# Storing the first block's results in 16 transfers instead of 64, and the last eight stores from two queues

## The chip, the cores and the metric

The kernel runs on one core of a Trainium2 chip. The metric is the device time of one execution in microseconds (us). TensorE (PE) multiplies matrices, VectorE (DVE) and ScalarE (ACT) do elementwise work and move results out of PSUM, GpSimd (POOL) does some additions, SyncE (SP) issues nearly all DMA transfers. An issue is an instruction in the queue of the engine that makes it: what stands behind it in that queue waits until it has been issued. The 16 DMA engines then move the bytes.

## The reference

Linear attention over 8 batches of 8 heads, an RMS norm, and two pairs of dense layers over the 4608 tokens, all in float32:

```python
kv = np.einsum('bhsd,bhse->bhde', k, v)          # batch 8, heads 8, seq 576, head_dim 64
out = np.einsum('bhsd,bhde->bhse', q, kv)
rms = np.sqrt(np.mean(out * out, axis=-1, keepdims=True) + 1e-06)
x = out / rms * g_norm                            # to [4608, 512]
h = x @ w_in                                      # [512, 2048]
x = where(h >= 1, h, where(h <= -1, 0, (h + 1) ** 2 / 4)) @ w_out
h = np.maximum(x @ w_in2, 0.0)
return (h * h) @ w_out2                           # [4608, 512]
```

The weights arrive in 64 bits and are narrowed to float32 on the chip.

## The kernel before

Every product is made of three products of rounded halves (a high and a low part, `mm3`, `mm_group`), so that float32 accuracy comes out of faster matmuls. The tokens are cut into nine blocks of 512: one of each batch (512 of its 576 rows), and block 8 of the 64 rows that are left of each batch.

The first layer pair runs block by block (`h_stage`, `g_stage`, `out_stage`). Its results go to DRAM tensors `x1d`. The second layer pair takes blocks 0 to 7 in four pairs, n = 0 to 3, each as a 2x2 product with seven instead of eight block products. A pair has two phases: `in_phase(n)` (tiles `ph`, 28 weight tiles, 12 matmuls each) and `out_phase(n)` (tiles `po`). Block 8 runs at the end like a block of the first layer pair.

The weight tiles of the second layer pair (`ws`, 512 KB each) are read from DRAM into a ring of eight buffers. `take_w2` takes a tile for the matmuls and calls `load_w2` (line 669), which issues the load seven tiles ahead on SyncE; the load waits until TensorE is through with the tile whose buffer it fills.

The results of a pair are stored while the next pair's `in_phase` runs: the list `late` has four calls of `put_out(n, hn, hm)`, which are made at steps 0, 1, 5 and 9 of that phase. `hn` says which block of the pair, `hm` which half of its 512 columns. Each call transposes two result tiles on DVE (line 885) into a tile `ov` and stores it from SyncE, 32 rows of output columns at a time. In block 0 the tokens stand in another order than in the others (row 4p + c of the batch is token p of group c, because its q, k and v were loaded that way), and so its stores differ: line 894 has 32 transfers of 16 KB for each call, line 901, for all other blocks, eight of 64 KB. The tile `ov` comes from `t_ring`, a ring of five buffers, of which `out_phase` takes its operands `t` as well: an operand that gets a buffer back from an `ov` waits until its stores have been written.

The order in each queue follows the program text, with a scheduler that moves instructions by their expected readiness; the names in the rows below are those of the tiles.

At the end, `out_stage(2, 8, 15)` copies four results from PSUM, two on DVE (line 601) and two on ACT (line 603), and each is stored in two halves of 64 rows by line 618 from SyncE.

Of the kernel before, what the change touches and what calls it, by code (L numbers as in the profile page):

```python
# [73 lines left out]
def linear_attention_rms_two_mlps(  # L74
# [12 lines left out]
    nc = tc.nc  # L87
    B, H, S, D = q.shape
    NT, DM = out.shape
    DFF = w_in1.shape[1] // 2  # L90
    P = 128
    NP = H // 2
    KD = DM // P
    NF = DFF // P
    TB = 512
    MR = TB // P
    REM = S - TB
    U = S // 2
    NB = NT // TB
# [88 lines left out]
    def mm3(dst, wt, xt, first, last):  # L188

        for n, (a, c) in enumerate(((0, 0), (0, 1), (1, 0))):  # L190
            nc.tensor.matmul(dst, wt(a), xt(c), start=first and n == 0, stop=last and n == 2)  # L191
# [391 lines left out]
    def out_stage(L, b, f):  # L583
        t = gs.pop((L, b, f))
        w = wo[L, f]
        if f == 0:
            acc[L, b] = [
                ps_a.tile([P, TB], F32, tag=f"acc{c}", name=f"acc{L}_{b}_{c}") for c in range(KD)
            ]
        for c in range(KD):  # L590
            s = slice(c * P, (c + 1) * P)
            if L == 1:
                lhs, rhs = (lambda a: w[:, a, s]), (lambda a: t[:, a, :])
            else:
                lhs, rhs = (lambda a: t[:, a, s]), (lambda a: w[:, a, :])
            mm3(acc[L, b][c], lhs, rhs, f == 0, f == NF - 1)
        if f == NF - 1:
            for c, a in enumerate(acc.pop((L, b))):
                t = st.tile([P, TB], F32, tag="st", name=f"ev{L}_{b}_{c}")
                if c % 2 == 0:  # L600
                    nc.vector.tensor_copy(t, a)
                else:
                    nc.scalar.copy(t, a)
                store(L, b, c, t)

    def store(L, b, c, t):
        if L == 1:
            nc.sync.dma_start(x1d[b][:, c, :], t)
        elif b == 0:

            nc.sync.dma_start(out[:TB, :].rearrange("(p c) f -> p c f", c=MR)[:, c, :], t)
        elif b < B:
            r0 = b * S + c * P
            nc.sync.dma_start(out[r0 : r0 + P, :], t)
        else:
            for j in range(P // REM):
                r0 = (c * (P // REM) + j) * S + TB
                nc.sync.dma_start(out[r0 : r0 + REM, :], t[j * REM : (j + 1) * REM, :])

    x_st = {}  # L620

# [257 lines left out]
    def put_out(n, hn, hm):  # L879


        t = t_ring.tile([P, 2, TB], F32, f"ov{n}_{hn}_{hm}")
        b = 2 * n + hn
        for m in range(2):
            nc.vector.transpose(t[:, m, :], result[n](hm, m, hn))
            d0 = (2 * hm + m) * P
            cols = out[b * S : b * S + TB, d0 : d0 + P]
            if b == 0:

                for c in range(MR):  # L890
                    for a in range(MR):
                        rows = cols.rearrange("(b i c) (a j) -> c a i b j", c=MR, i=32, j=32)
                        src = t[a * 32 : (a + 1) * 32, m, c * P : (c + 1) * P]
                        nc.sync.dma_start(  # L894
                            rows[c, a], src.rearrange("p (b j) -> p b j", j=32)
                        )
            else:
                for a in range(MR):
                    rows = cols.rearrange("(b i) (a j) -> a i b j", i=32, j=32)
                    src = t[a * 32 : (a + 1) * 32, m, :]  # L900
                    nc.sync.dma_start(rows[a], src.rearrange("p (b j) -> p b j", j=32))

    blocks = [(1, b) for b in range(NB)]
    hooks = {}
# [38 lines left out]
    for j in range(2 * NH):  # L943
        which, i = j % 2, j // 2
# [67 lines left out]
    for t in range(N1):  # L1012
        h_stage(*step(t))
        for f, a in hooks.get((t, 0), []):
            f(*a)
        g_stage(*step(t))
        if t >= LAG:
            out_stage(*step(t - LAG))
        for f, a in hooks.get((t, 1), []):
            f(*a)  # L1020

    late = []
    for n in range(NS):
        step_in = in_phase(n)
        for i, _ in enumerate(step_in):
            if n == 0 and i < LAG:
                out_stage(*step(N1 - LAG + i))
            if late and i in (0, 1, 5, 9):
                late.pop(0)()
        while late:  # L1030
            late.pop(0)()
        result[n] = result_of(dict(g2))
        jobs = x2_jobs(n + 1, tmp) if n + 1 < NS else x2_whole_jobs(2, NB - 1)
        at = range(8, 8 + 2 * len(jobs), 2)
        for _ in out_phase(n, jobs, at):
            pass
        late = [lambda n=n, h=h: put_out(n, h // 2, h % 2) for h in range(4)]

    L, b = 2, NB - 1
    for t in range(NF + LAG):  # L1040
        if t < NF:
            wi[L, t] = take_w2(0, t)
            h_stage(L, b, t)
        if late:
            late.pop(0)()
        if t < NF:
            g_stage(L, b, t)
        if t >= LAG:
            wo[L, t - LAG] = take_w2(1, t - LAG)
            out_stage(L, b, t - LAG)  # L1050
# [36 lines left out]
```

## Time and profile before

| | |
|---|---|
| median of 3 runs | 1629.64 us (1629.54 to 1631.46) |
| profiled execution | 1629.64 us, span from the first to the last instruction 1627.9 us |
| PE busy | 1593.7 us (98%), 7208 matmuls |
| DVE, ACT, POOL busy | 987.0 us (61%), 914.9 us (56%), 114.6 us (7%) |
| DMA | 302.31 MB, mean 186 GB/s |
| stores of line 901 | 112 of 64 KB, median 3.7 us from issue to landing |
| stores of line 894 | 64 of 16 KB, 1.5 us |
| stores of line 618 | 8 of 128 KB, 2.3 us |

Matmuls are pipelined, so the busy time of PE says that it hardly stands still, not how well it is used. Idle time of another engine costs nothing as long as PE does not wait for it. In the rows, `SPq` and `ACTq` are the queues of SyncE and ACT from which transfers are issued; the time beside such a row is that of the issue, and the landing is counted from its start.

### The profile page before, as it was taken

Reading aid. Unit: us, or ns where it says so; the run is one execution under the profiler, and the core shown is the slowest. Engines: PE = TensorE matmul, PEld = TensorE weight load, DVE = VectorE, ACT = ScalarE, POOL = GpSimd, SP = SyncE. Lnnn points to the kernel's source line nnn. Section 1 sums busy time; section 2 is a strip of 40 time slices with the busy share of each in tenths; the row PEclk is TensorE's granted clock in tenths of the full one; section 3 lists DMA queues with packets and bytes.
Section 4 is the critical chain, followed back from the end, with each engine's and each line's share of the span. In section 5 each row is a group of like instructions: output and inputs, shape, how many; then the busy total and the mean of one; then the engine's idle time right before and its main releaser. Section 6 shows DMA issues by size and latency. Waiting matters only on the chain.

```text
span 1627.9 us, 20609 instructions
## 1 busy us (share of the span) xinstructions
PE 1593.7 (98%) x7208; PEld 1312.0 (81%) x7208; DVE 987.0 (61%) x1638; ACT 914.9 (56%) x1661; POOL 114.6 (7%) x105
## 2 busy tenths in 40 slices
PE   8999999999999999999999999979999999999998
PEld 4778888888888888888888888868888888888886
DVE  6998665866757576443244348734875497457522
ACT  5777666766667666554344456436654664564321
POOL 0000000000000000000000121012101210230000
PEclk9999999999999999999999999989999999999999
DMA  9925668586667747313141457548758676865683
GB/s 264 276 93 156 212 182 263 161 251 184 196 198 223 231 148 238 112 56 104 39 144 38 156 194 245 194 119 257 246 192 225 208 241 198 241 220 184 193 246 102
DMA packets 307734, 302.31 MB, mean 186 GB/s; under 512 B 196272, under 2 KB 249520, under 8 KB 307632
## 3 DMA queue, kind: packets, MB, share of 16 engines
q1 hardware_dynamic: 305888, 300.61, 60.2%
q8 instruction: 57, 0.93, 0.2%
q10 hardware_dynamic: 1744, 0.39, 0.1%
q14 instruction: 45, 0.37, 0.1%
HBM read 231.74 MB, written 69.21 MB: 185 GB/s over the span
## 4 chain that ended last, share of the span: by engine, by line
PE 75%; issue 10%; DVE 9%; ACT 3%; DMA 1%; SPq 1%; POOL 1%; DVEq 0%; POOLq 0%; ACTq 0%
PE ph L191 26%; PE acc L191 25%; PE ph L737 11%; PE po L737 7%; DVE t L682 3%; PE pkv L403 2%; DVE x L682 1%; PE po L191 1%; PE pr L503 1%; SPq L894 1%; DVE g L827 1%; DMA ws<-wsd 1%; POOL t L798 1%; DVE xr L705 1%; DMA xr<-x1d 1%
## 5 line engine op out<-in xcount | busy, mean ns | idle before, releaser
L191 PE MATMUL ph<-x,w 128*128 128x512 f32 x1728 | 424.4, 394 | 9.5 <-ACT x L170 4.5
L191 PEld LDWEIGHTS ph<-x,w 128*128 128x128 f32 x1728 | 322.2, 189 | 78.9 <-ACT x L170 5.7
L737 PE MATMUL ph<-x,ws 128*128 128x512 f32 x1344 | 308.2, 391 | 11.0 <-DMA ws<-wsd 10.4
L737 PE MATMUL po<-t,ws 128*128 128x512 f32 x1344 | 307.4, 390 | 1.5 <-DVE t L682 1.5
L737 PEld LDWEIGHTS ph<-x,ws 128*128 128x128 f32 x1344 | 253.0, 189 | 65.2 <-issue 10.8
L737 PEld LDWEIGHTS po<-t,ws 128*128 128x128 f32 x1344 | 251.4, 188 | 56.9 <-DVE t L682 4.7
L191 PE MATMUL acc<-gs,w 128*128 128x512 f32 x1152 | 280.6, 391 | 0.3 <-DVE gs L184 0.2
L191 PEld LDWEIGHTS acc<-gs,w 128*128 128x128 f32 x1152 | 214.2, 188 | 44.4 <-DVE gs L184 1.4
L569 ACT ACTIVATE u<-ph,halfb 128x512 f32<-128x512 f32 x144 | 99.2, 689 | 205.1 <-PE ph L191 204.9
L571 DVE SCALAR_TENSOR_TENSOR u<-u,ph 128x512 f32<-128x512 f32 x144 | 98.6, 685 | 159.6 <-ACT u L178 158.9
L682 DVE TENSOR_TENSOR t<-g,t 128x512 fp32r<-128x512 f32 x192 | 135.3, 711 | 85.1 <-ACT t L170 69.3
L170 ACT CAST t<-g 128x512 fp32r<-128x512 f32 x192 | 116.4, 621 | 71.8 <-DVE t L682 50.1
L184 DVE TENSOR_TENSOR gs<-u,gs 128x512 fp32r<-128x512 f32 x160 | 110.4, 691 | 59.7 <-ACT gs L170 58.6
L191 PE MATMUL acc<-gs,wt 128*128 128x512 f32 x576 | 139.4, 391 | 0.0
L170 ACT CAST gs<-u 128x512 fp32r<-128x512 f32 x160 | 99.3, 621 | 69.7 <-DVE u L571 53.8
L191 PEld LDWEIGHTS acc<-gs,wt 128*128 128x128 f32 x576 | 106.8, 188 | 21.3
L790 DVE TENSOR_TENSOR h<-ph,e 128x512 f32<-128x512 f32 x96 | 66.1, 691 | 56.4 <-PE ph L737 50.7
L791 ACT ACTIVATE h<-h 128x512 f32<-128x512 f32 x96 | 60.5, 630 | 60.2 <-DVE h L790 56.0
L178 ACT ACTIVATE u<-u 128x512 f32<-128x512 f32 x144 | 91.0, 632 | 2.2
L798 POOL TENSOR_TENSOR t<-g 128x512 f32<-128x512 f32 x32 | 43.1, 1348 | 645.6 <-ACT g L792 365.0
L792 ACT ACTIVATE g<-h 128x512 f32<-128x512 f32 x128 | 80.9, 632 | 3.5
L782 DVE TENSOR_TENSOR e<-ph,e 128x512 f32<-128x512 f32 x64 | 43.4, 689 | 44.8 <-PE ph L737 43.7
(109 smaller groups left out, 1511.9 us busy)
## 6 DMA issues: line engine op xcount, KB each, us to landing
ws<-wsd SPq DMA_DIRECT2D x224, 512.0 KB, 3.4
wsd<-s SPq DMA_DIRECT2D x112, 256.0 KB, 3.9
wt<-wtd SPq DMA_DIRECT2D x48, 512.0 KB, 4.7
raw<-in_moe_w_in_dram SPq DMA_DIRECT2D x32, 512.0 KB, 5.2
raw<-in_moe_w_out_dram SPq DMA_DIRECT2D x32, 512.0 KB, 5.3
wcd<-s SPq DMA_DIRECT2D x32, 512.0 KB, 3.6
ws<-wcd SPq DMA_DIRECT2D x32, 512.0 KB, 4.3
x1d<-ev SPq DMA_DIRECT2D x36, 256.0 KB, 3.4
```

Source lines behind the costliest of these rows:

```text
L170: e.copy(dst, src)
L178: e.activation(dst, src, AF.Square)
L184: engine(op + "_lo", phase).tensor_tensor(t[:, 1, :], src, t[:, 0, :].bitcast(F32), ALU.subtract)
L191: nc.tensor.matmul(dst, wt(a), xt(c), start=first and n == 0, stop=last and n == 2)
L569: nc.scalar.activation(u, ps, AF.Relu, bias=halfb, scale=0.5)
L571: nc.vector.scalar_tensor_tensor(u, u, 1.0, ps, op0=ALU.min, op1=ALU.max)
L682: engine2(op + "_lo").tensor_tensor(t[:, 1, :], src, t[:, 0, :].bitcast(F32), ALU.subtract)
L737: nc.tensor.matmul(ps, wt(a), xt(c), start=first and n == 0 and i == 0, stop=last and n == len(lhs) - 1 and i == 2, skip_group_check=True,)
L790: nc.vector.tensor_tensor(h, bank, add, ALU.add)
L791: nc.scalar.activation(h, h, AF.Relu)
L792: nc.scalar.activation(g, h, AF.Square)
L798: engine2("t_sum").tensor_tensor(t1[k], b, a, ALU.subtract)
```

## The change

Block 0's stores are no longer split by token group: one transfer has the output rows of all four groups (`c`), as the other blocks' have, so that a call of `put_out` makes eight transfers of 64 KB. In the built program such a store is 128x4x32: 128 rows, four pieces in each, of 32 floats (128 bytes); line 901's stores are 32x16x32. The eight stores of block 8 are gathered in `last_out` and issued behind all four copies, five from SyncE and three from ACT.

```diff
-                store(L, b, c, t)
+                if (L, b) != (2, NB - 1):
+                    store(L, b, c, t)
+                else:
+                    last_out.append(t)
+
+            for c, j, e in LAST:
+                if last_out:
+                    r0 = (c * (P // REM) + j) * S + TB
+                    src = last_out[c][j * REM : (j + 1) * REM, :]
+                    e.dma_start(out[r0 : r0 + REM, :], src)
+
+    last_out = []
+    LAST = [
+        (c, j, nc.sync if c < 2 or (c, j) == (3, 0) else nc.scalar) for c in range(KD) for j in range(2)
+    ]
...
-            if b == 0:
-
-                for c in range(MR):
-                    for a in range(MR):
-                        rows = cols.rearrange("(b i c) (a j) -> c a i b j", c=MR, i=32, j=32)
-                        src = t[a * 32 : (a + 1) * 32, m, c * P : (c + 1) * P]
-                        nc.sync.dma_start(
-                            rows[c, a], src.rearrange("p (b j) -> p b j", j=32)
-                        )
-            else:
-                for a in range(MR):
+            for a in range(MR):
+                src = t[a * 32 : (a + 1) * 32, m, :]
+                if b == 0:
+
+                    rows = cols.rearrange("(b i c) (a j) -> a i c b j", c=MR, i=32, j=32)
+                    src = src.rearrange("p (c b j) -> p c b j", c=MR, j=32)
+                else:
                     rows = cols.rearrange("(b i) (a j) -> a i b j", i=32, j=32)
-                    src = t[a * 32 : (a + 1) * 32, m, :]
-                    nc.sync.dma_start(rows[a], src.rearrange("p (b j) -> p b j", j=32))
+                    src = src.rearrange("p (b j) -> p b j", j=32)
+                nc.sync.dma_start(rows[a], src)
```

SyncE's queue before, where the second pair's `in_phase` begins (`ws_1_6` is the ninth weight tile of the phase, `ws_1_2` the tenth; `ov_0_0` and `ov_0_1` are the two halves of block 0, `ov_1_0` is of block 1):

```order
L669 DMA ws_0_4_9495<-wsd_0_4_114 128x1024
L894 DMA out_dram<-ov_0_0_9552 32x4x32 x3
L669 DMA ws_0_3_9512<-wsd_0_3_115 128x1024
L894 DMA out_dram<-ov_0_0_9552 32x4x32 x2
L669 DMA ws_1_1_9528<-wsd_1_1_116 128x1024
L894 DMA out_dram<-ov_0_0_9552 32x4x32 x27
L669 DMA ws_1_6_9587<-wsd_1_6_117 128x1024
L894 DMA out_dram<-ov_0_1_9607 32x4x32 x32
L669 DMA ws_1_2_9642<-wsd_1_2_118 128x1024
```

The same place after the change:

```order
L679 DMA ws_0_4_9495<-wsd_0_4_114 128x1024
L907 DMA out_dram<-ov_0_0_9552 128x4x32
L679 DMA ws_0_3_9512<-wsd_0_3_115 128x1024
L907 DMA out_dram<-ov_0_0_9552 128x4x32
L679 DMA ws_1_1_9528<-wsd_1_1_116 128x1024
L907 DMA out_dram<-ov_0_0_9552 128x4x32 x6
L679 DMA ws_1_6_9563<-wsd_1_6_117 128x1024
L907 DMA out_dram<-ov_0_1_9583 128x4x32 x8
L679 DMA ws_1_2_9594<-wsd_1_2_118 128x1024
```

Between the loads of the eighth (`ws_1_1`) and the ninth tile 6 stores stand instead of 27, and 8 instead of 32 ahead of the tenth. In the phases of the third and the fourth pair the same numbers of stores of line 901 stand there, before and after.

DVE in that phase before; the `h` rows add PSUM tiles of products 4 and 3, `t_1_1` is an operand for the phase after:

```order
L790 TENSOR_TENSOR h_4_0_9712<-ph_6_0_9589,e_1_0_9537 128x512
L790 TENSOR_TENSOR h_4_1_9722<-ph_6_1_9598,e_1_1_9548 128x512
L790 TENSOR_TENSOR h_3_0_9745<-ph_5_0_9682,e_1_0_9596 128x512
L682 TENSOR_TENSOR t_1_1_10247<-g_1_1_0_9549,t_1_1_10247 128x512
L790 TENSOR_TENSOR h_3_1_9755<-ph_5_1_9693,e_1_1_9605 128x512
```

And after the change:

```order
L692 TENSOR_TENSOR t_1_1_10199<-g_1_1_0_9549,t_1_1_10199 128x512
L800 TENSOR_TENSOR h_4_0_9664<-ph_6_0_9565,e_1_0_9537 128x512
L800 TENSOR_TENSOR h_4_1_9674<-ph_6_1_9574,e_1_1_9548 128x512
L800 TENSOR_TENSOR h_3_0_9697<-ph_5_0_9634,e_1_0_9572 128x512
L800 TENSOR_TENSOR h_3_1_9707<-ph_5_1_9645,e_1_1_9581 128x512
```

`t_1_1` stands three instructions earlier, as it does in the third pair's phase; its rounding on ACT moved with it.

The end of ACT's queue after the change (before, it ended with the two copies, and all eight stores stood in SyncE's):

```order
L170 CAST gs_8_15_14045<-u_8_15_14042 128x512
L603 COPY ev_8_1_14086<-acc_8_1_13589 128x512
L603 COPY ev_8_3_14090<-acc_8_3_13591 128x512
L613 DMA out_dram<-ev_8_2_14088 64x512 x2
L613 DMA out_dram<-ev_8_3_14090 64x512
```

Both halves of the third result and one of the fourth are issued behind ACT's last copy in its queue; SyncE keeps both halves of the first two and the other half of the fourth.

## Rows read from the trace of the kernel before

**Rows 1.** Waits of TensorE, 850 us to the end: who, for whom, total us, times, longest.

```profile
PE ph L737 <- DMA ws<-wsd: 10.4, 1, 10.4
```

**Rows 2.** Chain of waits, 1074 to 1098 us: start us, us, what.

```profile
1090.56 0.43 SPq L894
...
1091.08 4.49 DMA ws<-wsd
...
1095.71 2.47 PE ph L737 x5
```

**Rows 3.** Timeline of SyncE, 1040 to 1110 us: start us, us, what, how many.

```profile
1061.27 12.92 SPq L894 DMA_DIRECT2D out_dram<-ov  x27
1074.29 1.21 SPq L669 DMA_DIRECT2D ws<-wsd  x1
1075.60 15.38 SPq L894 DMA_DIRECT2D out_dram<-ov  x32
```

**Rows 4.** Windows, three phases: us; PE, PEld, DVE, ACT, POOL busy; PEclk, DMA, GB/s.

```profile
1060.69:1149.41 88.72, 78.12 (x338) 63.96 (x336) 35.68 (x54) 44.30 (x74) 17.86 (x12) 0.94 0.63 190
1226.41:1303.08 76.67, 76.45 (x337) 62.99 (x336) 35.69 (x54) 44.30 (x74) 17.90 (x12) 1.00 0.76 220
1380.09:1456.77 76.68, 76.46 (x338) 62.98 (x336) 35.69 (x54) 43.94 (x73) 17.91 (x12) 1.00 0.76 220
```

**Rows 5.** Windows of line 737 alone: us; PE, PEld busy; granted clock, DMA, GB/s.

```profile
1095.70:1098.70 3.00, 2.99 (x7) 2.42 (x8) 0.50 0.96 327
1098.70:1101.40 2.70, 2.70 (x13) 2.21 (x13) 1.00 0.77 134
```

**Rows 6.** Timeline of SyncE, 1221 to 1262 us, in the third pair's phase.

```profile
1226.97 3.73 SPq L901 DMA_DIRECT2D out_dram<-ov  x6
...
1231.36 5.09 SPq L901 DMA_DIRECT2D out_dram<-ov  x8
1236.55 3.97 SPq L669 DMA_DIRECT2D ws<-wsd  x4
```

**Rows 7.** All issues into the output: ns shortest/median/longest, first and last start.

```profile
L901 SPq DMA_DIRECT2D out_dram<-ov x112: 337/510/2820, 1093.0 to 1557.6; - x112
...
L894 SPq DMA_DIRECT2D out_dram<-ov x64: 315/430/564, 1056.2 to 1090.6; - x64
```

**Rows 8.** Waits of DVE, 1050 to 1150 us, then 1220 to 1300 us.

```profile
DVE t L682 <- DMA out_dram<-ov: 15.2, 2, 13.4
...
DVE t L682 <- DMA ws<-wsd: 0.5, 1, 0.5
```

**Rows 9.** Timelines of the end: SyncE alone, then all engines.

```profile
1619.99 5.01 SPq L618 DMA_DIRECT2D out_dram<-ev  x8
...
1620.63 0.69 DVE L601 COPY ev<-acc 128x512 f32<-128x512 f32 x1 [0.67 <-PE acc L191]
1621.31 0.59 ACT L603 COPY ev<-acc 128x512 f32<-128x512 f32 x1 [0.77 <-PE acc L191]
```

**Rows 10.** Line 618, the last eight stores: us from issue to landing.

```profile
DMA to landing us min/median/max: 2.3/2.3/2.4
```

**Rows 11.** Line 389, three of ACT's loads at the start: us from issue to landing.

```profile
DMA to landing us min/median/max: 4.3/4.9/5.9
```

**Rows 12.** Windows, the last stores: columns as in rows 4.

```profile
1621.20:1626.30 5.10, 0.07 (x1) 0.00 (x0) 0.12 (x1) 0.59 (x1) 0.00 (x0) 0.81 0.89 205
```

**Rows 13.** Timeline of all engines, 0 to 4 us.

```profile
0.73 1.28 ACT L968 ACT_TABLE_LOAD   x1 [0.73 <-PEq L1065]
...
0.73 0.77 SPq L347 DMA_DIRECT2D k<-in_k_dram  x1
0.76 0.75 ACTq L389 DMA_DIRECT2D kvr<-in_k_dram  x1
...
2.48 0.66 ACTq L389 DMA_DIRECT2D qr<-in_q_dram  x1
...
2.95 0.71 SPq L347 DMA_DIRECT2D k<-in_k_dram  x1
```

More of the change, by code (lines that the diff above doesn't have):

```diff
@@ L611, in store @@
             nc.sync.dma_start(out[:TB, :].rearrange("(p c) f -> p c f", c=MR)[:, c, :], t)
-        elif b < B:
+        else:
             r0 = b * S + c * P
             nc.sync.dma_start(out[r0 : r0 + P, :], t)
-        else:
-            for j in range(P // REM):
-                r0 = (c * (P // REM) + j) * S + TB
-                nc.sync.dma_start(out[r0 : r0 + REM, :], t[j * REM : (j + 1) * REM, :])
     x_st = {}
@@ L887, in put_out @@
             cols = out[b * S : b * S + TB, d0 : d0 + P]
-            if b == 0:
-                for c in range(MR):
-                    for a in range(MR):
-                        rows = cols.rearrange("(b i c) (a j) -> c a i b j", c=MR, i=32, j=32)
-                        src = t[a * 32 : (a + 1) * 32, m, c * P : (c + 1) * P]
-                        nc.sync.dma_start(
-                            rows[c, a], src.rearrange("p (b j) -> p b j", j=32)
-                        )
-            else:
-                for a in range(MR):
+            for a in range(MR):
[3 more added lines that the diff above has]
+                    src = src.rearrange("p (c b j) -> p c b j", c=MR, j=32)
+                else:
                     rows = cols.rearrange("(b i) (a j) -> a i b j", i=32, j=32)
-                    src = t[a * 32 : (a + 1) * 32, m, :]
-                    nc.sync.dma_start(rows[a], src.rearrange("p (b j) -> p b j", j=32))
+                    src = src.rearrange("p (b j) -> p b j", j=32)
+                nc.sync.dma_start(rows[a], src)
     blocks = [(1, b) for b in range(NB)]
```

## The prediction

> **What bounds the kernel now.** I read the page first: TensorE is busy for nearly the whole span, so only a place where it stands still, or the tail behind its last matmul, can give time back. The next view is TensorE's waits over the second half of the program: a single wait counts, 10.4 us of the matmuls into `ph` for a weight tile [rows 1]. The chain of waits says what made that tile late: up to 1090.56 the chain runs through stores of line 894, one after another, then a weight load that is issued at 1091.08 and takes 4.49 us to land, then the matmul at 1095.71 [rows 2]. SyncE's timeline shows the queue it stood in: 27 stores in 12.92 us, one load, 32 stores in 15.38 us [rows 3]. Both sets of stores write block 0's results, and the load of the tenth weight tile of the stage is behind them in program order.
>
> What that costs in all is read by stage. Phase 1 of the strip products (the matmuls into `ph` of the second pair of blocks) lasts 88.72 us. The same phase of the third and the fourth pair, with the same 28 weight tiles, matmuls and work of DVE and POOL, lasts 76.67 and 76.68 us [rows 4]. The difference is 12.05 us. Two parts of it are visible: the idle time itself, and seven matmuls behind it that took 3.0 us at a granted clock of 0.50 (the 1.2 GHz level, after some 10 us without a matmul) where 13 take 2.70 us at 1.00; seven at that pace are 1.45 us, so 1.5 us went there [rows 5]. 10.4 + 1.5 = 11.9 us, and 0.1 is spread over small gaps.
>
> **Part one: 16 stores for 64.** The number of issues in front of the tenth tile falls, and each moves four times as many bytes, in runs of the same 128 bytes. The profile has a direct relative: in the phase of the third pair, 16 stores of line 901 (64 KB, 512 runs each) stand at exactly the places at which the 16 new ones will stand, with the same loads between them. There, 6 stores take 3.73 us and 8 take 5.09, and the tenth tile's load is issued at 1236.55 [rows 6]: 10.14 us after that phase began at 1226.41. At a landing time of 4.49 it is there at 14.6 us. It is wanted after nine tiles, 9 x 76.67 / 28 = 24.6 us. So the cover is 10.0 us: the 14 stores, 8.8 us now, could take 18.8, or 1.34 us each, before TensorE waits at all. The same sum for today's phase: issued 30.4 us after 1060.69, landed at 34.9, wanted at 24.6, late by 10.3. It reproduces the wait.
>
> What a store of 128x4x32 runs costs to issue is not in this trace. From below: line 894's median, 430 ns for 128 runs. From above: line 901's longest, 2820 ns for 512 runs, issued straight behind four weight loads [rows 7]. I take line 901's 0.63 us per store of the burst, since runs, bytes, source layout and neighbours in the queue are equal, and only the step between runs in DRAM differs. The Trainium skill bears on this (Perfetto Trace Analysis, section DMA Instruction — HWDGE (DVE, Sync)): what the profile shows of a DMA instruction is lock wait, descriptor generation and the push of its semaphore, not the data movement. If generation were all of it, four times the runs would take four times as long; the trace does not bear that out, 510 ns median against 430.
>
> On DVE one instruction moves: the subtraction into `t_1_1`, which waits for the first result tile's stores to leave its buffer, goes ahead of three more `h` additions, the place that its sister has in the third pair's phase. Behind it queue the additions that empty PSUM, and TensorE waits for those. Today such waits are 15.2 us in two; in the third pair's phase the one wait is 0.5 us [rows 8], and no wait of TensorE follows from it, since that phase has the undisturbed length. So it is priced at nothing, under cover of the stores' 0.63 us; if they are slow, it goes with the rival below.
>
> So the phase should take 76.7 us: **-12.05 us**. Next late is nothing that the third and fourth pair do not also have.
>
> **Part two: the last eight stores.** Today eight issues follow each other from 1619.99 for 5.01 us, 0.63 each, while the last results leave DVE at 1621.32 (1620.63 + 0.69) and ACT at 1621.90 (1621.31 + 0.59) [rows 9]. The eighth begins at about 1624.4 and lands 2.4 us later, 1626.8 [rows 10]; the span ends 1.1 us behind that. Now SyncE has five, of which the fifth begins at 1619.99 + 4 x 0.63 = 1622.5 and lands at 1624.9. ACT has three: they begin between 1621.35 (at the start ACT's queue issues at 0.76 beside a table load that its engine works on from 0.73 for 1.28 us [rows 13]) and 1621.95 (behind its last copy); the third, two issues later, begins at 1622.6 to 1623.2 and lands by 1625.0 to 1625.6. That is 1.2 to 1.8 us earlier. Three reasons to take less: where both queues issue at once, at the program's start, an issue takes 0.66 to 0.77 us, and seven issues (four of SyncE, three of ACT) take from 0.73 to 3.66, 0.42 each [rows 13], which lets the last of the six from 1621.27 on begin at about 1623.1 and land at 1625.5; the DMA engines show a share of 0.89 at 205 GB/s during these stores [rows 12], so that overlapping transfers may slow each other; and ACT's queue has issued nothing since the start. The low end is no gain: the pace of 0.63 is then that of the transfers. Below nothing lies ACT's landing time at the start, 4.3 to 5.9 us [rows 11]: 1623.2 + 5.9 = 1629.1, a loss of 2.3. I take **-1.1 us**, between none and 1.8 and near the pace of two queues.
>
> The Trainium skill has a rule against this half (same page and section): the descriptor generator is shared by the sequencers and locked for one instruction at a time. By it the eight issues follow each other as today and the half gives 0. The trace does not agree fully, as 0.42 us per issue on two queues is under the 0.6 of one.
>
> **Sum.** The profiled execution took 1629.64 us (span 1627.9), which is also the median of the runs, so nothing is rescaled. 1629.64 - 12.05 - 1.1 = **1616.5 us**.
>
> **Rivals.**
> - The tail gives nothing (generator or transfers are the limit): 1629.64 - 12.05 = 1617.6. For it the share of 0.89; against it the pace at the start. Chance 0.20. That ACT's late landing makes it a loss, up to 1619.9: 0.05.
> - Issue time grows with the runs: 4 x 430 = 1720 ns. 14 stores take 24.1 us instead of 8.8, the tenth tile's load goes out at 10.14 + 15.3 = 25.4, lands at 29.9, and TensorE idles 5.3 us, with up to 1.5 us of low clock: 1621.7 to 1623.2. Line 901 speaks against it. Chance 0.06.
> - No change: at 28.3 us for the 14 stores (12.92 + 15.38 today), 2.02 us each, the wait is as long as now; 1628.5. Chance 0.04 for about there.
> - Slower: the step between runs makes the queue back up so that every store takes line 901's longest time. 14 x 2.82 = 39.5 us, load at 40.8, landed at 45.3, idle 20.7 us, 10.3 more than today: 1638.8. It decides from 2.02 us per store on, and DVE's moved wait would lengthen with it. For it: line 901's spread, from a median of 510 ns to 2820. Against it: the first 14 of the third pair's phase, 8.82 us together. Chance 0.03.
> - That the change does not do what it says is excluded by the order of instructions, which has 16 stores and five plus three.
>
> **How the numbers follow.** The forecast has 0.62, with 1615.7 to 1617.6 as its own range (tail 1.8 to 0, plus the spread of runs). With the tail's cases 0.87 lie below 1620; the range gives up the last of them above, and reaches 0.7 us under the best tail for the spread between runs: 1615.0 to 1619.6. Under 0.2% (3.3 us) this kernel's runs can't tell a change from none. Faster by more: 0.62 + 0.20 + 0.05 + 0.06 = 0.93; within: 0.04; slower: 0.03.
>
> **What would show it.** Right: no wait of TensorE for a weight tile; granted clock 1.00 throughout that phase, length 76.7; 16 stores of line 907 for block 0 at 0.4 to 0.7 us mostly; the tenth tile's load some 10 us into the phase; the last store landed some 13.1 us earlier than at 1626.8, and the span 13.1 us shorter. Wrong: stores above 1.34 us each and a wait for `ws` in that phase; a DVE wait for stores of several us followed by one of TensorE; in the tail, ACT's three issues not overlapping SyncE's, or landing over 2.6 us after their start.

## The result, and the profile after

The changed kernel takes 1616.62 us (median of four runs, 1616.36 to 1616.93) beside 1630.15 us before (four runs, 1629.54 to 1631.46): a ratio of 0.9916 with a 95% interval of 0.9899 to 0.9933, or 13.5 us. The forecast was 1616.5. The profiled execution took 1616.48 us with a span of 1614.7, 13.2 us less than the span before, and the trace tells where these 13.2 went. I divided both spans at the same places: the beginning and the end of the second pair's `in_phase`, and the first of the last eight stores.

| stretch | before | after | difference |
|---|---|---|---|
| start to that phase | 1060.69 | 1060.50 | -0.19 |
| the phase | 88.72 | 76.68 | -12.04 |
| from it to the first last store | 470.58 | 470.56 | -0.02 |
| from there to the end | 7.91 | 6.96 | -0.95 |

Windows of the kernel after, the phase, the same phase of the third pair, and the tail (us; PE, PEld, DVE, ACT, POOL busy; PEclk, DMA, GB/s):

```profile
1060.50:1137.18 76.68, 76.46 (x338) 63.02 (x336) 35.69 (x54) 44.29 (x74) 17.90 (x12) 1.00 0.75 220
1214.37:1291.04 76.67, 76.45 (x337) 63.02 (x336) 35.46 (x53) 44.51 (x74) 17.89 (x12) 1.00 0.74 218
1607.74:1614.70 6.96, 1.29 (x6) 0.74 (x4) 0.69 (x1) 1.14 (x2) 0.00 (x0) 0.80 0.55 151
```

The second pair's phase is now as long as its sisters, and the granted clock in it is 1.00 (the 2.4 GHz level) instead of 0.94 on average [rows 4]. The waits of TensorE over the second half show why:

```profile
PE po L747 <- DVE t L692: 1.6, 4, 0.9
PE ph L747 <- DVE e L792: 0.7, 3, 0.2
```

The wait of 10.4 us for a weight tile [rows 1] is gone, and nothing has come in its place; the two others were there before the change:

```profile
PE po L737 <- DVE t L682: 1.5, 4, 0.8
PE ph L737 <- DVE e L782: 0.7, 3, 0.2
```

SyncE's timeline in the second pair's phase, to be read beside [rows 3, 6]:

```profile
1061.06 4.63 SPq L907 DMA_DIRECT2D out_dram<-ov  x6
1065.79 0.56 SPq L679 DMA_DIRECT2D ws<-wsd  x1
1066.45 5.54 SPq L907 DMA_DIRECT2D out_dram<-ov  x8
1072.10 2.52 SPq L679 DMA_DIRECT2D ws<-wsd  x4
```

The 14 stores take 10.17 us where 59 took 28.30, and the tenth tile's load goes out 11.6 us after the phase began instead of 30.4. The issues of the 16 new stores by themselves (ns shortest/median/longest, first and last start):

```profile
L907 SPq DMA_DIRECT2D out_dram<-ov x16: 590/628/1287, 1056.0 to 1071.4; - x16
```

Four times as many runs cost a median of 628 ns instead of 430 [rows 7]. DVE's waits between 1050 and 1150 us no longer hold the 15.2 us for stores [rows 8]; of waits for a DMA one is left, and TensorE waits for DVE in that phase for 0.2 us at the longest:

```profile
DVE t L692 <- DMA ws<-wsd: 1.9, 1, 1.9
```

The tail on all engines, to be read beside [rows 9]:

```profile
1607.74 3.11 SPq L613 DMA_DIRECT2D out_dram<-ev  x5
1608.38 0.69 DVE L601 COPY ev<-acc 128x512 f32<-128x512 f32 x1 [0.67 <-PE acc L191]
1609.06 0.58 ACT L603 COPY ev<-acc 128x512 f32<-128x512 f32 x1 [0.77 <-PE acc L191]
1609.12 2.01 ACTq L613 DMA_DIRECT2D out_dram<-ev  x3
```

ACT's first issue stores the third result, which DVE has copied by 1609.07; it begins at 1609.12, while ACT's engine is still at the copy that stands ahead of it (1609.06 to 1609.64). All eight issues are out 3.39 us after the first one began, where they took 5.01. The stores' landing times by queue, SyncE's first and then ACT's (us from issue to landing, shortest/median/longest):

```profile
DMA to landing us min/median/max: 2.3/2.4/3.2
...
DMA to landing us min/median/max: 3.0/3.0/3.2
```

Alone on their queue all eight landed after 2.3 to 2.4 us [rows 10].

### The profile page after: what moved, and what is told of

Read it like the earlier page. It is cut to its first block, busy times and chain, and to the rows that moved or that the text cites. A ratio compares the mean times of both kernels' runs of the same rounds, so it can differ in the third digit from the quotient of the medians.

```text
span 1614.7 us, 20560 instructions
## 1 busy us (share of the span) xinstructions
PE 1589.9 (98%) x7207; PEld 1310.6 (81%) x7208; DVE 987.0 (61%) x1638; ACT 914.3 (57%) x1661; POOL 114.6 (7%) x105
## 4 chain that ended last, share of the span: by engine, by line
PE 70%; issue 14%; DVE 11%; ACT 2%; POOL 1%; DMA 1%; DVEq 0%; SPq 0%; POOLq 0%; ACTq 0%
PE ph L191 26%; PE acc L191 26%; PE ph L747 10%; PE po L747 4%; DVE t L692 4%; PE pkv L403 2%; DVE x L692 2%; PE po L191 1%; POOL t L808 1%; PE pr L503 1%; DVE g L837 1%; DVE xr L715 1%; DVE d L223 1%; DVE w L184 1%; DVE d L226 1%
## 5 line engine op out<-in xcount | busy, mean ns | idle before, releaser
L191 PE MATMUL ph<-x,w 128*128 128x512 f32 x1728 | 422.2, 393 | 10.2 <-ACT x L170 4.5
L191 PEld LDWEIGHTS acc<-gs,wt 128*128 128x128 f32 x576 | 106.9, 188 | 21.3
```

## The experiments

The theory: what cost 12 us was the number of issues ahead of the tenth load in SyncE's own queue, and the tail gains what a second queue's issues overlap, less what overlapping transfers lose. The rivals: the size and the form of the small stores cost as such; all queues' issues take turns at one unit; the tail is bound by its transfers.

### Each part alone

`e1_part_one` has the first part of the diff only, `e2_part_two` the second only.

> Only block 0's 16 stores; the last eight stores as in the kernel before, all from SyncE. Theory (the two parts are independent, and part one is worth the whole wait for the tenth weight tile with the low clock behind it): second pair's in_phase 76.7 us, span from the first of the last eight stores to the end 7.9 us as before, time 1630.15 - 12.05 = 1618.1 against the mean of the runs before, or 1617.6 against the profiled execution: 0.9 to 1.1 us above the changed kernel. Rival (the tail's part is worth nothing, and the changed kernel's last us came from somewhere else): the same time as the changed kernel, 1616.6.

> Only the tail: the last eight stores gathered, five from SyncE and three from ACT; block 0 keeps its 64 stores. Theory: in_phase of the second pair stays at 88.7 us with its wait of 10.4 us, from the first of the last stores to the end 7.0 us instead of 7.9; 0.9 us faster than before, about 1629.2. Rival (tail worth nothing): 1630.15, 7.9 us at the end. Rival (lock of the issue path): SyncE's and ACT's issues follow each other, none overlapping.

Part one alone: 1618.6 us (1616.71 to 1619.08, five runs; ratio 0.9923, interval 0.9909 to 0.9936). Part two alone: 1629.65 us (1628.01 to 1630.11, 11 runs; ratio 0.9992, 0.9983 to 1.0001), beside 1630.37 us before. By time alone part two can't be told from nothing. The windows show it: the phase, then the tail, of part one alone and of part two alone.

```profile
1061.04:1137.71 76.67, 76.45 (x338) 62.99 (x336) 35.70 (x54) 44.30 (x74) 17.91 (x12) 1.00 0.75 220
1608.97:1616.80 7.83, 1.28 (x6) 0.74 (x4) 0.69 (x1) 1.14 (x2) 0.00 (x0) 0.75 0.57 134
```

```profile
1061.09:1150.35 89.26, 78.96 (x338) 64.54 (x336) 35.69 (x54) 44.41 (x74) 17.88 (x12) 0.94 0.63 189
1621.05:1628.00 6.95, 1.28 (x6) 0.74 (x4) 0.69 (x1) 1.14 (x2) 0.00 (x0) 0.87 0.56 151
```

Each part does its work without the other: 76.67 us in the phase with part one, 6.95 us at the end with part two, and the other stretch as before (7.83 and 89.26, against 7.91 and 88.72). The sum of both is the changed kernel. The execution of part one alone also began its phase 0.5 us later and had 0.7 us more between phase and tail than the changed kernel's, which is why its time is 2 us above the changed kernel's and not 0.9: stretches that the change does not touch differ by that much between executions.

### Is it the number of issues, or the stores' size?

`e4_extra48` makes 64 issues of the 16 again, by additional stores of 4 KB; `e5_extra16` makes 32.

```diff
+                if b == 0:
+                    for _ in range(EXTRA):      # 3 in e4_extra48, 1 in e5_extra16
+                        nc.sync.dma_start(pads.pop(), t[a * 32 : (a + 1) * 32, m, :32])
```

> The changed kernel with three additional stores of 4 KB (32 rows of 128 bytes into scratch) behind each of block 0's 16: 64 issues again, as before the change, with 0.2 MB more bytes. Theory (issues in the queue count): 42 of the 48 stand ahead of the tenth tile's load; at 0.315 to 0.43 us each that is 13.2 to 18.1 us, of which the unused cover hides 8.5: TensorE waits 4.7 to 9.6 us for the tenth tile, with up to 1.5 us of low clock: 1621.3 to 1627.7. Rival (the gain is due to fewer, larger transfers at the DMA engines): the bytes rise by a fifth of block 0's stores only, no wait: 1616.6.

> The changed kernel with one additional store of 4 KB (into scratch) behind each of block 0's 16 stores: 32 issues. In e4_extra48 such a store held the queue for some 0.53 us. Theory (issues ahead of the tenth load count, and the first 10 us of them are free): 14 more issues, 14 x 0.53 = 7.4 us, under the 8.5 us of cover that are left: no wait of TensorE for a weight tile, phase 76.7 us, time that of the changed kernel: 1616.6. Rival (each issue more costs time in proportion, as 42 cost 15.3 us of wait): 14 / 42 of it, 5.1 us: 1621.7.

With 48 additional stores: 1634.42 us (1632.04 to 1636.98, ten runs; ratio 1.0025, 1.0016 to 1.0034), slower than the kernel before, with 0.2 MB more to move. With 16: 1616.33 us (1615.82 to 1618.32, five runs), as fast as the changed kernel. In the first, TensorE's wait for the tile is back, longer than in the kernel before:

```profile
PE ph L749 <- DMA ws<-wsd: 15.3, 1, 15.3
```

SyncE's timeline there shows one of the 16 stores (L909) with its three additional ones (L912), and the tenth tile's load behind all of them:

```profile
1093.79 0.60 SPq L909 DMA_DIRECT2D out_dram<-ov  x1
1094.42 1.54 SPq L912 DMA_DIRECT2D pad<-ov  x3
1096.07 1.79 SPq L681 DMA_DIRECT2D ws<-wsd  x4
```

A store of 4 KB with 32 runs takes 0.51 us of the queue, one of 64 KB with 512 runs some 0.63. So between 4 and 64 KB bytes and runs hardly count, issues do. The time is above the range that I wrote down for two reasons: I had mis-sized the additional stores (0.315 to 0.43 us, so a wait of 4.7 to 9.6), and in this phase 46 of them and 15 of the 16 stand ahead of the load, where I had counted 42 and 14. The sign and the place are the theory's. The execution with 16 additional stores is the other test, of the cover: its phase is undisturbed,

```profile
1060.19:1136.90 76.71, 76.65 (x337) 62.91 (x336) 35.69 (x54) 44.35 (x74) 17.92 (x12) 1.00 0.71 219
```

although the tenth tile's load goes out at 1080.85, 20.7 us after the phase began and 9.1 us later than in the changed kernel:

```profile
1080.85 1.79 SPq L681 DMA_DIRECT2D ws<-wsd  x4
```

The runs in which the loads stand in the old order lie on one line. The prediction put the latest harmless issue at 24.6 - 4.49 = 20.1 us into the phase:

| kernel | tenth load issued, us into the phase | TensorE's wait for it |
|---|---|---|
| changed kernel | 1072.10 - 1060.50 = 11.6 | none |
| e1_part_one | 1073.69 - 1061.04 = 12.7 | none |
| e5_extra16 | 1080.85 - 1060.19 = 20.7 | none |
| e9_alternate (below) | 1083.00 - 1061.72 = 21.3 | none, 2.3 for ACT at that place |
| before | 1091.08 - 1060.69 = 30.4 | 10.4 |
| e2_part_two | 1092.12 - 1061.09 = 31.0 | 10.1 |
| e4_extra48 | 1096.07 - 1059.57 = 36.5 | 15.3 |

Issue less wait is 20.0 to 21.2 in the last three, and at 20.7 e5_extra16 still has no wait. What differs is the landing of that load: it took 4.5, 3.6 and 3.3 us in the last three, and issue plus landing less wait is 24.5 us in each, where the prediction wants the tile (24.6). In e5_extra16 it landed after 3.2 us, at 23.9, and so in time.

### The same 64 stores, elsewhere

`e3_spread` has every store of the kernel before, but calls `put_out` later, and `e9_alternate` leaves them in place and issues every second one from ACT:

```diff
-            if late and i in (0, 1, 5, 9):
+            if late and i in (0, 6, 10, 13):
```

```diff
-                        nc.sync.dma_start(
+                        (nc.sync if a % 2 == 0 else nc.scalar).dma_start(
```

> The kernel before with its 64 stores, but the four calls of put_out made at steps 0, 6, 10 and 13 of the next phase instead of 0, 1, 5 and 9, so that loads of weight tiles stand between the 27 and the 32 stores of block 0. Theory (the loads are late because of what stands ahead of them in SyncE's queue, 59 issues in a row but for one load): each group of 27 or 32 stores takes 13 to 15.4 us of the queue by itself, of which some 14.5 us are covered by the ring, so that TensorE waits 0 to 1 us: 1617.6 to 1619.5, most of the 12 us back without any change of a store. Rival (the small stores as such are the cost, by their bytes or their short runs at the DMA engines, wherever they stand): the wait stays near 10 us, 1629 to 1630. The calls of the other pairs move too; a new wait of DVE for their buffers would show as time above 1619.5.

> The kernel before with its 64 stores and all else in place, but every second one issued from ACT's queue instead of SyncE's: 27 stores instead of 59 stand ahead of the tenth tile's load in SyncE's queue. Theory (what delays the load is its own queue): 27 x 0.48 = 13 us, load issued some 14 us into the phase, under the cover: no wait for a weight tile, 1617.6 to 1618.6 as with part one alone, plus what ACT's 32 issues (0.48 us each, up to 15 us of its queue in the first 25 us of the phase) delay of its copies out of PSUM: 0 to 6 us. Rival (issues of all queues take turns at one shared unit): both queues together still need 0.48 us per issue, the load goes out as late as before, wait near 10 us: 1629 to 1631.

Spread: 1622.12 us (1621.16 to 1625.02, four runs; ratio 0.9951, 0.9937 to 0.9964). Most comes back with no store changed, so the small stores' bytes as such are out as the cause. But a wait of 3.0 us is left where I expected 0 to 1:

```profile
PE ph L737 <- DMA ws<-wsd: 3.0, 1, 3.0
```

SyncE's timeline says why (the 27 stores, the loads between, the 32 stores, and the loads that are late):

```profile
1060.81 14.22 SPq L894 DMA_DIRECT2D out_dram<-ov  x27
1075.12 3.18 SPq L669 DMA_DIRECT2D ws<-wsd  x6
1078.39 18.92 SPq L894 DMA_DIRECT2D out_dram<-ov  x32
1097.41 1.80 SPq L669 DMA_DIRECT2D ws<-wsd  x4
```

The 32 stores take 18.92 us behind six loads of 512 KB, 3.5 us more than the 15.38 that I had carried over from [rows 3]. The waits of SyncE's queue between 1078 and 1097.3 us name what they wait for, a wait that the kernel before does not have there:

```profile
SPq L894 <- DMA ws<-wsd: 4.2, 5, 1.1
```

In the built program each transfer takes one of eight semaphores in turn, and waits until the transfer that had it before has landed (the second and the third store of that place, with the semaphores that they wait for):

```
L894 DMA out_dram<-ov_0_1_9713 32x4x32 [waits DMAHW6_49]
L894 DMA out_dram<-ov_0_1_9713 32x4x32 [waits DMAHW7_49]
```

So the third to eighth store behind the six loads come eight places after a load, and with 4.2 us of such waits taken off, the 32 stores are 14.7 us, as expected. I had not counted these semaphores. A wait of 3.0 us also brings the low clock again: the windows of TensorE's matmuls right behind it (us; PE, PEld busy; granted clock, DMA, GB/s) have 6 in 2.56 us at 0.50 and 13 in 3.00 us at 0.88, against 13 in 2.70 at 1.00 in [rows 5].

```profile
1101.44:1104.00 2.56, 2.56 (x6) 2.08 (x7) 0.50 0.96 352
1104.00:1107.00 3.00, 3.00 (x13) 2.40 (x13) 0.88 1.00 220
```

The phase is 80.94 us: 76.67, 2.97 of wait, and 1.30 of low clock.

Alternating: 1622.99 us (1621.09 to 1625.33, four runs; ratio 0.9952, 0.9935 to 0.9969). The wait for the weight tile is gone, though only just: its load landed after 3.4 us, at 1086.4, when TensorE was through with the nine tiles ahead of it (1061.72 + 24.64). A wait for ACT has come, the one wait of TensorE in that phase over 0.3 us:

```profile
PE ph L737 <- ACT e L775: 2.3, 1, 2.3
```

ACT copies results out of PSUM (line 775). Its timeline has the 18 stores that it issues in a row, and the copy that TensorE waited for:

```profile
1067.68 11.02 ACTq L894 DMA_DIRECT2D out_dram<-ov  x18
1088.04 1.05 ACT L775 COPY e<-ph 128x512 f32<-128x512 f32 x2
```

What stood behind the stores in ACT's queue, activations and casts, runs from 1078.74 on without a break, and the copy comes behind it at 1088.04; in the kernel before, these two copies began at 1081.29 and 1082.65. The whole phase:

```profile
1061.72:1142.73 81.01, 78.50 (x337) 63.81 (x336) 37.47 (x54) 42.84 (x74) 17.66 (x12) 0.98 0.72 212
```

It is 81.01 us: 76.67, 2.30 of wait, and 2.05 in which the same matmuls were slower (PE busy 78.50 for 76.45, at a granted clock of 0.64 to 0.74 behind the wait). Over the whole phase each queue took more per store than the 0.48 us of SyncE alone (15.38 / 32): SyncE's last 16 took 10.12 us, ACT's last 18 took 11.02. That looks like two queues that slow each other, but SyncE's waits from 1064 to 1083 us say otherwise:

```profile
SPq L894 <- DMA out_dram<-ov: 3.5, 5, 2.3
SPq L894 <- DMA ws<-wsd: 2.5, 1, 2.5
```

It is the semaphores again, which both queues share and which now wait for landings of the other queue's transfers and of the loads. Where neither waits, from 1070.2 to 1072.6 us, the issues of ACT and of SyncE are these:

```profile
L894 ACTq DMA_DIRECT2D out_dram<-ov x6: 322/442/447, 1070.1 to 1072.4; - x6
L894 SPq DMA_DIRECT2D out_dram<-ov x4: 315/420/433, 1070.3 to 1071.6; - x4
```

ACT begins five issues more in the 2.3 us behind its first, 0.46 each, and SyncE three in 1.3 us, 0.43 each, at the same time: both at the pace of one queue alone. The rival by which issues take turns is out.

### The tail

`e6_halves` issues the first half of each last result from SyncE and the second from ACT; `e7_halves2` does so behind each pair of copies; `e8_small_tail` is the changed kernel with a quarter of the bytes in these stores. The core of e7_halves2 and that of e8_small_tail:

```diff
+                if c % 2 == 1:
+                    for c2 in (c - 1, c):
+                        for j, e in enumerate((nc.sync, nc.scalar)):
```

```diff
-                    src = last_out[c][j * REM : (j + 1) * REM, :]
-                    e.dma_start(out[r0 : r0 + REM, :], src)
+                    src = last_out[c][j * REM : (j + 1) * REM, :128]
+                    e.dma_start(out[r0 : r0 + REM, :128], src)
```

> The changed kernel with the eight last stores left in place behind their copies, the first half of each result from SyncE and the second from ACT (four and four); in ACT's queue the second half of the third result stands ahead of the copy of the fourth. Theory (two queues issue side by side, about 0.55 us an issue each): the last result's copy is some 0.5 us late, but the last issue begins at about the same time and overlaps with one transfer instead of three: 6.0 to 6.6 us from the first store to the end instead of 7.0, 1615.6 to 1616.2. Rival (issues share one unit, 0.6 us each): 7.0 to 8 us, not faster than 1616.6.

> As e6_halves, but each pair of results is stored behind both of its copies, so that ACT's order is copy, two issues, copy, two issues, and SyncE has four. Theory (two queues side by side): the last issue begins at some 1609.8 to 1610.2 by the clock of the changed kernel instead of 1610.58 and lands by 1612.5 to 1613.1: 0.5 to 1.1 us faster than the changed kernel, 1615.5 to 1616.1, and the fastest kernel here. Rival (the DMA engines' pace for stores of 64 rows is the limit, whoever issues): 1 MB at some 205 GB/s takes 5.1 us from the first store on, as before the change: no gain, 1616.6.

> The changed kernel with the last eight stores cut to the first 128 of 512 columns (32 KB instead of 128 KB each; the rest of block 8's output is not written). It asks what the lengthened landing of ACT's stores (3.0 us where SyncE's alone took 2.3) comes from. Theory (the bytes of two queues in flight at once): issues as long as now, 0.5 to 0.6 us, but every landing 1.6 to 2.1 us and none longer for ACT's: 0.9 to 1.3 us faster, about 1615.5. Rival (ACT's queue itself lands late, or two issuing engines delay each other's completion): ACT's landings stay 0.5 us or more above SyncE's first one, and the end comes less than 0.6 us earlier.

Times: 1616.4 (1615.84 to 1617.75), 1616.14 (1615.85 to 1616.22) and 1615.43 us (1614.89 to 1617.38). The windows from the first of the last stores to the end, one kernel each, are the better ruler, beside 6.96 for the changed kernel:

```profile
1608.16:1614.60 6.44, 1.28 (x6) 0.74 (x4) 0.69 (x1) 1.13 (x2) 0.00 (x0) 0.96 0.52 163
```

```profile
1607.98:1614.30 6.32, 1.28 (x6) 0.74 (x4) 0.69 (x1) 1.13 (x2) 0.00 (x0) 0.85 0.52 166
```

```profile
1607.76:1613.60 5.84, 1.28 (x6) 0.74 (x4) 0.69 (x1) 1.13 (x2) 0.00 (x0) 0.92 0.17 45
```

Four and four is 0.5 to 0.6 us better than five and three, inside what I expected of both, though both times are at or just above the upper end that I wrote down. The shorter stores end 1.1 us sooner, also as expected. With a quarter of the bytes the issues are as long as with all of them, and the landings of both queues fall together. Of e8_small_tail, ACT's issues and their landings:

```profile
L613 ACTq DMA_DIRECT2D out_dram<-ev x3: 517/559/802, 1609.1 to 1610.6; - x3
...
DMA to landing us min/median/max: 1.9/2.0/2.1
```

So ACT's 3.0 us in the changed kernel are neither ACT's queue as such nor the issuing; they are the bytes of two queues in flight at once. The DMA engines are no hard limit at 205 GB/s either, which was the rival's number. The view of the DMA engines from 1607 to 1615 us in the changed kernel gives, in 40 slices of 0.2 us, their busy share in tenths and the GB/s; where both queues' stores are in flight it reaches 410:

```profile
DMA  0000000002988987897899799999992000000000
GB/s 0 0 0 0 0 0 0 0 0 72 225 195 195 236 195 174 226 225 174 215 184 205 205 410 389 277 307 359 348 358 72 0 0 0 0 0 0 0 0 0
```

The share is 0.7 to 0.9 in the slices of 174 to 236 GB/s and 0.9 in those of 277 to 410, so the share of 0.89 before the change [rows 12] did not mean that the engines could move no more.

To see whether 0.6 us in the trace is also 0.6 us on the clock, both kernels ran once more on one chip.

> The changed kernel again, on one chip with e11_halves2_again, since a difference of 0.6 us is less than what runs of different calls differ by. Theory (the tail of e7_halves2 is really shorter): 7.0 us from the first of the last stores to the end here, 6.3 there, and the medians 0.4 to 1.0 us apart. Rival (the gain in the profile is one execution's): medians within 0.3 us.

> The kernel of e7_halves2 again, beside e10_after_again. Theory: 6.3 us from the first of the last stores to the end, 0.4 to 1.0 us under the median of e10_after_again. Rival: within 0.3 us of it.

The medians are 1617.04 (1616.54 to 1618.54, four runs) and 1616.67 us (1615.53 to 1617.65, five): 0.37 apart, between the two expectations, with ranges that overlap. In the trace the tails are 6.93 and 6.29 us, the same 0.64 as the first time:

```profile
1609.87:1616.80 6.93, 1.28 (x6) 0.74 (x4) 0.69 (x1) 1.13 (x2) 0.00 (x0) 0.93 0.56 151
```

```profile
1607.41:1613.70 6.29, 1.28 (x6) 0.74 (x4) 0.69 (x1) 1.13 (x2) 0.00 (x0) 0.93 0.52 167
```

So e7_halves2 has the shorter tail, shown twice in the trace, and its times alone do not prove a faster kernel. The start of the program differs by more than the tails: in these two executions the granted clock of the first 100 us was 0.93 and 0.98 on average, and the second pair's phase began at 1062.35 and 1059.93, 2.4 us apart.

## Why the prediction was right

**What bounds the kernel.** The place, the cause and the price held. The phase fell by 12.04 us where 12.05 was taken from its sisters [rows 4], and part one alone does it. That the queue's order is the cause, which the prediction read from the chain and the timeline [rows 2, 3], is now shown from four sides: fewer issues, additional issues, the same issues later, and half of them in another queue.

**The price of a store.** It was a little too low, and did not matter. I took 0.63 us for each of the burst; the first six take 0.77 us (4.63 / 6) and the next eight 0.69 (5.54 / 8), 1.35 us more in all than in [rows 6]. The cover of 10.0 us took it up, and e5_extra16 shows that the cover is at least as large as the sum said. That is why the forecast could rest on a store's price known only between 0.43 and 2.82: the answer is flat up to 1.34 us, and for the price to lie below that the prediction had line 901's stores. One reading behind the upper bound was not exact: the store of 2820 ns [rows 7] begins at 1106.89 and is the fifth behind four weight loads, not the first.

**Runs.** The Trainium skill (Perfetto Trace Analysis, section DMA Instruction — HWDGE (DVE, Sync)) reads a DMA instruction's profiled time as lock wait, descriptor generation and semaphore push. If generation were all of it, the time would go with the runs; that rival did not come true: 32 runs take 0.42 us (the median of e4_extra48's additional stores), 512 take 0.63.

**DVE's moved instruction.** Priced at nothing, and nothing came of it: DVE's waits for stores went from 15.2 us to none, and TensorE's waits for DVE in that half of the program are 0.2 us and 0.9 us at the longest.

**The tail.** The term of 1.1 us measured 0.95. Its issuing half came out as written: SyncE's fifth issue began 2.6 us after its first (predicted 2.5), ACT's third 2.9 us after it (2.6 to 3.2), and eight issues took 0.42 us each, the pace of two queues at the start [rows 13]. (An issue took 0.63 to 0.91 us there, and not 0.66 to 0.77 as the prediction read it; the pace of 0.42 stands.) The landing half did not: 2.4 us was carried over from stores that one queue issues [rows 10], and with two queues' transfers in flight it was 2.8 to 3.2. Landings of over 2.6 us were among the prediction's own signs of being wrong, and this one came; it cost some 0.6 us at the last store. The term is off by only 0.15 us because it had been taken below the 1.2 to 1.8 us that the issues gave, and the transfers' mutual slowing was one of the reasons; e8_small_tail shows that this reason was right, while the size of the discount was a guess.

The Trainium skill (Perfetto Trace Analysis, section DMA Instruction — HWDGE (DVE, Sync)) has the rule that the descriptor generator is locked for one instruction at a time, which would have made this half 0 if the lock lasted for a whole issue. The traces do not bear that out for two engines: the tail's 0.42 us per issue is under the 0.55 that one issue takes there, and in e9_alternate two queues ran at 0.46 and 0.43 us side by side, each as fast as one alone. A lock for a smaller part of an issue is not excluded by these runs.

**The rest.** 0.19 us came before the phase, from the start, whose length differs by more than that between executions of one kernel. That forecast and median agree to 0.1 us is luck: the tail and the start were each off by 0.15 to 0.19 us, in opposite directions, and the median of the same kernel in e10_after_again is 1617.04.

## What to carry to other kernels

When a load is late, look at what stands ahead of it in its own queue and count the issues, not the bytes: from 4 to 64 KB a store cost its issue here, and 14 stores of 64 KB took 10.2 us of the queue where 59 of 16 KB took 28.3. Work out how late a load may go out before anybody waits: as long as the new price is under that point, it need not be known well. A second issuing queue runs beside the first at full pace, as these runs show it for SyncE and ACT, but its issues stand in line with that engine's own work, and a copy that others wait for should not be behind a row of them.

## What the runs showed of the hardware

- A sixteenth of the bytes did not make an issue much shorter. A store of 4 KB (32 runs of 128 bytes) took 0.42 us in the median and 0.51 from one to the next; one of 64 KB (512 runs) 0.60 to 0.63. Straight behind a 64 KB store a 4 KB store took 0.61 us (the median of e5_extra16, and the first of the last three in e4_extra48, whose other two took 0.42), as if an issue also paid for the one ahead of it; why is open.
- Two queues issued stores of 16 KB side by side at 0.46 and 0.43 us each, against 0.48 in one alone. What slowed them elsewhere was the program's eight semaphores: a store waits for the transfer eight places ahead of it, 4.2 us in five waits behind six loads of 512 KB (e3_spread), up to 2.5 us for one load (e9_alternate).
- ACT's queue began an issue 0.06 us after its engine had begun the copy that stood ahead of it, and was through with it (0.50 us) by the copy's end. An instruction behind stores does wait for their issues: in e9_alternate a copy of ACT began at 1065.29, when the 13 ahead of it had been issued (1057.22 + 8.02).
- The granted clock was 0.50 (the 1.2 GHz level) behind 3.0 us without a matmul in e3_spread, as it was behind 10.4 us in the kernel before. What the phase took beyond 76.67 us and the wait did not follow the length of the wait: 2.05 us behind 2.3 (e9_alternate, where the clock was 0.64 to 0.74), 1.3 behind 3.0 (e3_spread), 2.5 behind 10.1 (e2_part_two), 1.7 behind 10.4 (before) and 1.9 behind 15.3 (e4_extra48).
